# Background products in halves of 64 rows beside the scores, transfers issued at due times, and the end of the program on other engines

## The chip, the cores and the metric

One Trainium2 core runs the program. TensorE (PE in the rows) multiplies, with its weight loads shown apart as PEld; VectorE (DVE), ScalarE (ACT) and GpSimd (POOL) work beside it, and SyncE (SP) issues every transfer from one in-order queue. The metric is the device time of one execution in microseconds, lower is better.

## The reference

One transformer block with adaptive layer norm over 2048 rows of width 512 in float32. `mod` is cut into six rows of 512.

```python
mod = (silu(c) @ w_mod).reshape(1, 6, 1, -1)
sa, ca, ga, sb, cb, gb = (mod[:, i] for i in range(6))
h = layernorm(x) * (1 + ca) + sa
x = x + ga * A(h)     # 32 heads of 16: softmax(q k^T / 4) v, then @ wo
h = layernorm(x) * (1 + cb) + sb
x = x + gb * B(h)     # gelu_tanh(h @ w1 + b1) @ w2 + b2, w1 512 x 1792
```

## The kernel before

Projections keep float32 accuracy by three products of split operands (high x high, low x high, high x low, `terms3`), each 128x128 weights by 512 columns in the one-pass float32 format. A prologue takes the modulation, the first norm, the values and the first part of queries and keys. q and k go through HBM as high and low parts and come back with a head in 48 rows, two heads of a group in rows 0 to 47 and 64 to 111. Two more rows hold the row maximum, so that `e` comes out shifted.

The scores loop runs over 32 units `u` (4 query blocks of 512 by 8 groups of 4 heads) of 16 key chunks, 512 steps in all. A step has four `exp_mm` (L533: `e`, 50 rows on one half of the array, to banks 0 to 2; ScalarE's exponential, L539, empties them) and four `mx_mm` (L375: scores with query rows out, on the other half, to banks 3 to 5; VectorE's maximum, L380, empties them), which run 96 products ahead for the maxima of the next units. `max_rows` (L386) turns a unit's maxima and sends them through `m_d` (L394) into the rows of `qst`. `pv_step` (L555) multiplies with the values in four tiles of 32 columns side by side into bank 6. The order is written out by hand: CYCLE has 12 `Y` (an `e` and an `mx`), three `p` (a `pv` step) and two `b` (background products).

Background products (L283, bank 7, 128 rows) come from generators: `block0`, the remaining q and k projections with `load_w` and `split_w` of their weights, then `ffn_block` for each query block: 4 groups of 12 products with `wo`, norm, transposes, 14 `ffn1` groups of 12 with a GELU written out on GpSimd around a tanh on ScalarE, and `ffn2` groups. `bg` issues four or six at a time:

```python
            elif o == "b":
                nb += 1
                bg(6 if work and len(work) <= NB and nb % 2 else 4)
```

`prep` splits the weights of the feed-forward part and stores them in HBM during the first units. `o_prep` (L584) divides a finished part of the attention by its sums: load `dn` and `ob`, reciprocal, store, load `rb` over the rows, multiply and split on GpSimd. `later(n, f)` calls `f` at the n-th tick; one tick is one `Y`, or after the loop three background products. A transfer stands in SyncE's queue where the program text issues it, and waits there for its data. After the loop the last query block's `ffn_block` runs alone.

## Time and profile before

| | |
|---|---|
| median of 3 runs | 2231.18 us (2221.09 to 2232.93) |
| profiled execution | 2227.8 us, span 2225.6 us, mean granted clock 0.917 |
| TensorE busy | 1925.6 us, 87% |
| VectorE busy | 1412.5 us, 63% |
| ScalarE busy | 1235.2 us, 56% |
| GpSimd busy | 751.7 us, 34% |
| transfers | 242.45 MB |

Busy time of TensorE counts overlapping products once. Where the engine waits and for whom is read by stage: prologue to 161.54 us (first `e`), loop to 2012.20 us (last `pv`), end of the program to 2225.60 us.

### The profile page before, as it was taken

To read this page: it belongs to the slowest core of one execution; us is meant where nothing else is said; L and a number is where in the kernel's file an instruction comes from. 1 tells how busy PE (TensorE), PEld (TensorE's weight loads), DVE (VectorE), ACT (ScalarE), POOL (GpSimd) and SP (SyncE) were. 2 spreads that over 40 slices of the span, in tenths; PEclk is the share of its full clock that TensorE was granted. 3 is DMA by queue.
4 is the path that set the end of the run, shared out by engine and by line. 5 is a ranking of instruction groups with operands and counts; after the bars stand their busy time and mean duration, and the time that the engine had idled before them with its cause. 6 is when DMAs were issued, how large, how long until landed. Compare 5 with 4: busy or idle time off the path is not lost.

```text
span 2225.6 us, 29467 instructions
## 1 busy us (share of the span) xinstructions
PE 1925.6 (87%) x10544; PEld 855.4 (38%) x10544; DVE 1412.5 (63%) x2317; ACT 1235.2 (56%) x2302; POOL 751.7 (34%) x787
## 2 busy tenths in 40 slices
PE   7899949898799898999979999999889999995566
PEld 5543313343233343433333333333333334333344
DVE  4476727687578777777767777778687777601000
ACT  2316637576466675767556766656557667571110
POOL 3313332321100451523302523414215415151886
PEclk8998969999789999999989999999899999996777
DMA  7554665556323443424443434333542524123221
GB/s 231 157 137 126 177 182 141 175 141 191 78 59 76 94 92 88 105 63 85 96 145 81 84 80 120 83 82 80 182 101 52 113 78 101 43 69 136 92 95 47
DMA packets 123919, 242.45 MB, mean 109 GB/s; under 512 B 32134, under 2 KB 51606, under 8 KB 123774
## 3 DMA queue, kind: packets, MB, share of 16 engines
q1 hardware_dynamic: 123774, 240.57, 41.5%
q8 instruction: 84, 1.38, 0.3%
q14 instruction: 61, 0.50, 0.1%
HBM read 187.61 MB, written 52.90 MB: 108 GB/s over the span
## 4 chain that ended last, share of the span: by engine, by line
PE 67%; DMA 10%; POOL 8%; DVE 6%; ACT 4%; issue 3%; SPq 2%; POOLq 0%; DVEq 0%; ACTq 0%
PE pv L562 20%; PE bg L283 19%; PE e L533 18%; PE mx L375 8%; DVE mxp L380 3%; PE pr L283 2%; DMA wf<-in_B_w_dram 2%; DMA w<-w1s 2%; ACT p L539 1%; DMA dn<-ou 1%; DMA wraw<-in_A_wqkv_dram 1%; DVE y L712 1%; DMA rden<-dn 1%; POOL h L692 1%; ACT h L683 1%
## 5 line engine op out<-in xcount | busy, mean ns | idle before, releaser
L380 DVE TENSOR_REDUCE mxp<-mx 128x1 f32<-128x512 f32 x2048 | 1298.8, 685 | 449.4 <-PE mx L375 388.4
L539 ACT ACTIVATE p<-e 128x512 f32<-128x512 f32 x2048 | 1092.7, 599 | 611.4 <-PE mx L375 399.9
L375 PE MATMUL mx<-kh,qst 48*128 48x512 f32 x2048 | 742.3, 459 | 51.1 <-DVE mxp L380 45.9
L533 PE MATMUL e<-qst,kh 50*128 50x512 f32 x2048 | 733.5, 453 | 15.4 <-ACT p L539 14.4
L562 PE MATMUL pv<-p,vg 128*32 128x512 f32 x4096 | 577.0, 637 | 6.2 <-ACT osb L548 6.2
L533 PEld LDWEIGHTS e<-qst,kh 50*128 50x128 f32 x2048 | 329.8, 192 | 616.3 <-ACT p L539 465.1
L375 PEld LDWEIGHTS mx<-kh,qst 48*128 48x128 f32 x2048 | 326.3, 192 | 88.6 <-DVE mxp L380 76.0
L283 PE MATMUL bg<-w,g 128*128 128x512 f32 x672 | 212.3, 443 | 89.1 <-POOL g L693 47.9
L283 PE MATMUL bg<-pc,w 128*128 128x512 f32 x672 | 193.8, 420 | 26.3 <-ACT h L683 16.3
L283 PEld LDWEIGHTS bg<-w,g 128*128 128x128 f32 x672 | 124.4, 201 | 168.8 <-POOL g L693 53.3
L713 POOL TENSOR_TENSOR x<-x,y 128x512 f32<-128x512 f32 x48 | 61.4, 1282 | 295.7 <-DVE y L712 295.6
L562 PEld LDWEIGHTS pv<-p,vg 128*32 128x32 f32 x4096 | 82.5, 110 | 198.2 <-issue 180.2
L283 PEld LDWEIGHTS bg<-pc,w 128*128 128x128 f32 x672 | 118.4, 191 | 94.2 <-issue 34.0
L712 DVE TENSOR_TENSOR y<-bg,gb_b 128x512 f32<-128x512 f32 x48 | 32.9, 685 | 181.3 <-PE bg L283 176.8
L691 POOL TENSOR_TENSOR u<-u,h 128x512 f32<-128x512 f32 x56 | 71.8, 1283 | 136.7 <-ACT u L689 136.7
L684 POOL TENSOR_TENSOR u<-h 128x512 f32<-128x512 f32 x56 | 58.3, 1041 | 112.7 <-ACT h L683 112.5
L599 POOL TENSOR_TENSOR ob<-ob,rb 128x512 f32<-128x512 f32 x16 | 20.4, 1274 | 224.4 <-DMA rb<-rden 205.3
L283 PE MATMUL bg<-wo,pc 128*128 128x512 f32 x192 | 60.9, 449 | 37.7 <-POOL pc L600 24.0
L683 ACT ACTIVATE h<-bg,b_h 128x512 f32<-128x512 f32 x56 | 38.7, 691 | 97.4 <-PE bg L283 80.3
L283 PE MATMUL bg<-hThi,wqk 128*128 128x512 f32 x176 | 59.0, 460 | 34.7 <-ACT wqk L163 23.3
L686 POOL TENSOR_TENSOR u<-u,h 128x512 f32<-128x512 f32 x56 | 71.7, 1281 | 4.7
L692 POOL TENSOR_TENSOR h<-u,h 128x512 f32<-128x512 f32 x56 | 71.6, 1278 | 4.4
(100 smaller groups left out, 949.9 us busy)
## 6 DMA issues: line engine op xcount, KB each, us to landing
kh<-qk SPq DMA_DIRECT2D x366, 128.0 KB
w<-w1s SPq DMA_DIRECT2D x56, 512.0 KB
w<-w2s SPq DMA_DIRECT2D x56, 512.0 KB
vg<-v SPq DMA_DIRECT2D x32, 664.0 KB
qk<-parts SPq DMA_DIRECT2D x32, 512.0 KB
qst<-qk SPq DMA_DIRECT2D x192, 64.0 KB
ou<-osb SPq DMA_DIRECT2D x32, 256.0 KB
wo<-wos SPq DMA_DIRECT2D x16, 512.0 KB
```

The source lines that it names most:

```text
L283: te.matmul(ps, p, q, start=i == 0, stop=i == len(terms) - 1)
L375: te.matmul(ps, qst[u][r0 : r0 + KR, p, qc * P : (qc + 1) * P], kh(u, kr // 2)[r0 : r0 + KR, p, (kr % 2) * TB : (kr % 2 + 1) * TB], start= ...
L380: ve.tensor_reduce(mxp[u][:, hc, kr : kr + 1], ps, axis=AX.X, op=ALU.max, negate=True)
L533: te.matmul(ps, kh(u, kc // 8)[r0 : r0 + KX, p, (kc % 8) * P : (kc % 8 + 1) * P], qst[u][r0 : r0 + KX, p], start=True, stop=True)
L539: ac.activation(pt[n], ps, AF.Exp, scale=SCALE)
L562: te.matmul(cur["ps"][32 * j : 32 * (j + 1)], vg[u][:, kc, j * VW : j * VW + 32], pt.pop(4 * s + j), start=kc == 0, stop=kc == NKC - 1)
L683: ac.activation(h, ps, AF.Identity, scale=0.5, bias=b1_h[:, i : i + 1])
L684: gp.tensor_tensor(s, h, h, op=ALU.mult)
L686: gp.tensor_tensor(s, s, h, op=ALU.mult)
L691: gp.tensor_tensor(s, s, h, op=ALU.mult)
L692: gp.tensor_tensor(h, s, h, op=ALU.add)
L713: gp.tensor_tensor(x2[t], x2[t], y, op=ALU.add)
```

## The change

A background product is cut into two products of 64 rows (`bg_mm`) that add to the same bank. In `half_step`, one per step, six of them on half `h` alternate with scores on the other half, three `mx` and three `e`; then one pair of an `e` and an `mx`, then one `pv` step. The half changes with each step, and a group of 12 products takes four steps. As both halves add to one bank, the first product on the other half is made to wait (`add_manual_dep`) for the first ScalarE exponential or copy that was issued after the last one of the old half (`saw`). CYCLE and `bg` go. A tick is now one `e`, or one pair before the loop, or two products after it.

The weights of the last two q and k parts are loaded and split inside `block0`, in two buffers in place of three. The stores of parts, maxima, weights, attention and output, and the steps of `o_prep`, get due times by `later`. `w2` is stored times `gb`, so the multiplication on VectorE and the addition on GpSimd become one addition on VectorE. The weight ring has 8 buffers and reloads a slot when its tile has been used; the exponential's tiles are 12 in place of 9.

After the loop seven banks hold background groups. What is left of the third block's work alternates with the last block, which has tiles of its own, prepares its attention output on VectorE, two parts at a time, and takes GELU as one ScalarE function with VectorE's subtraction for the low part.

```diff
-CYCLE = ("Y", "Y", "Y", "p", "Y", "Y", "b", "Y", "Y", "Y", "b", "Y", "Y", "p", "Y", "Y", "p")
-PARTS = ((0, 5), (5, 10), (10, NF))
-MM = "mm"
+AFTER = mybir.DependencyInfo(mybir.DependencyClass.Sync, mybir.DependencyReason.DATA)
+RUN = 6
+WB = 8
+PARTS = ((0, 6), (6, 12), (12, NF))
+AHEAD = 2
+GELU_A = 0.7978845608028654
+GELU_C = 4 * 0.044715
...
+    def mm(ps, term, i, n, r=slice(None)):
+        return te.matmul(ps, term[0][r], term[1][r], start=i == 0, stop=i == n - 1)
+
...
-            store_qk(w, k, b, parts)
+            if bk == "bg":
+                later(8, lambda: store_qk(w, k, b, parts))
+            else:
+                store_qk(w, k, b, parts)
...
-        sy.dma_start(m_d[u], m2.bitcast(F32))
...
+        def load():
+            mrows.add(u)
...
+        later(5, lambda: sy.dma_start(m_d[u], m2.bitcast(F32)))
+        later(11, load)
...
-    ppcm, ppool = pool("p", bufs=9)
+    ppcm, ppool = pool("p", bufs=12)
...
-    wcm2, wpool2 = pool("wqk2", side="right")
-    wq.append(wpool2.tile([P, 2, 2, KC, P], FR, name="wqk2"))
-    load_w(2)
-    split_w(2)
...
-            sy.dma_start(dst, t.bitcast(F32))
-
-        return rest
+            later(7, lambda: sy.dma_start(dst, t.bitcast(F32)))
+
+        later(11, rest)
...
-        preps.append((w2[f * P : (f + 1) * P, :], w2_d[f], None))
+        preps.append((w2[f * P : (f + 1) * P, :], w2_d[f], gb_b))
...
+    def exp_mm(a):
+
+        s, p = divmod(ec[a], 2)
...
+        ec[a] += 1
...
+            t = ppool.tile([P, TB], F32, tag="p", name="p")
+            saw(ac.activation(t, ps, AF.Exp, scale=SCALE))
+            pt[4 * s + p * 2 + a] = t
+            advance()
...
+        saw(ac.activation(o, pv, AF.Copy))
+        later(2, lambda: sy.dma_start(ou_d[qb][g], o))
...
+            later(8, lambda: ready.append((qb, g // 2)))
...
+        tgt = pools["pc"][k] if b < NB - 1 else pools["tail"]["pc"][k]
+        eng = gp if b < NB - 1 else ve
+        r = rden_d[b][k * 8 : (k + 1) * 8]
+        busy[0] += 1
+
+        def inv():
...
+            later(1, store)
+
+        def store():
+            sy.dma_start(r.rearrange("h (a f) -> (h a) f", f=32), dn)
+            later(4, load)
+
+        def load():
+            sy.dma_start(rb, bass.AP(tensor=r.tensor, offset=r.offset, ap=[[TB, 8], [0, DH], [1, TB]]))
+            later(4, div)
...
         def div():
-            ve.reciprocal(dn, dn)
-            sy.dma_start(rden_d[b][k * 8 : (k + 1) * 8].rearrange("h (a f) -> (h a) f", f=32), dn)
-            r = rden_d[b][k * 8 : (k + 1) * 8]
...
-            gp.tensor_tensor(ob, ob, rb, op=ALU.mult)
-            gp.tensor_copy(tgt[:, 0], ob)
-            gp.tensor_tensor(tgt[:, 1], ob, tgt[:, 0].bitcast(F32), op=ALU.subtract)
-            done[b] = k
-            busy[0] = False
-
-        busy[0] = True
-        later(8, div)
+            eng.tensor_tensor(ob, ob, rb, op=ALU.mult)
+            eng.tensor_copy(tgt[:, 0], ob)
+            eng.tensor_tensor(tgt[:, 1], ob, tgt[:, 0].bitcast(F32), op=ALU.subtract)
+            done[b] += 1
+            busy[0] -= 1
+
+        later(5, inv)
...
+        if not ready or "f" not in pools:
+            return
+        last = ready[0][0] == NB - 1
+        if "tail" in pools if last else free_pc[0] >= ready[0][0]:
+            if busy[0] < 1 + last:
+                o_prep(*ready.pop(0))
+
+    def until(cond):
+        while not cond():
+            yield None
+
+    def wait(n):
+        t0 = clock["t"]
+        return until(lambda: clock["t"] >= t0 + n)
...
+    def ffn_block(b):
...
+        def wload():
+            while n[0] < len(seq) and (n[0] < WB or seq[n[0] - WB] in used):
+                key = seq[n[0]]
+                t = f.tile([P, 2, D], FR, tag="w", name=f"w{key[0]}", bufs=WB)
...
+        if not tail:
+            wload()
...
-        while done[b] < KC - 1:
-            yield lambda: done[b] == KC - 1
-        t0 = clock["t"]
-        yield lambda: clock["t"] >= t0 + 12
+        yield from until(lambda: done[b] == KC - 1)
+        yield from wait(5)
...
+            yield [(pc[i][:, a, sl], wt["o", i][:, w]) for i in range(KC) for a, w in three], "bg", evac
+        if not tail:
+            used.update(seq[:KC])
+            wload()
+        yield from wait(2)
...
+        yield from wait(2)
...
+        yield from wait(4)
...
+            h = tmp("h32")
...
+            eng = ve if tail and fc % 2 else gp
+            eng.tensor_copy(pc[fc][:, 0], h)
+            eng.tensor_tensor(pc[fc][:, 1], h, pc[fc][:, 0].bitcast(F32), op=ALU.subtract)
+
+        for fc in range(KC):
+            yield lambda fc=fc: trans(fc)
+        if tail:
+            yield "ffn"
+            wload()
+        else:
+            yield from wait(4)
...
+            def evac_tail(ps):
+                h = tmp("h")
+                ac.activation(h, ps, AF.Gelu_apprx_tanh, bias=b1_f[:, i : i + 1])
+                g = f.tile([P, 2, TB], FR, tag="g", name="g", bufs=8)
+                ac.activation(g[:, 0], h, AF.Copy)
+                ve.tensor_tensor(g[:, 1], h, g[:, 0].bitcast(F32), op=ALU.subtract)
+                gt[i] = g, clock["t"] - 9
...
 
                 def second():
...
+                    ac.activation(s, s, AF.Tanh, scale=2 * GELU_A)
+                    g = f.tile([P, 2, TB], FR, tag="g", name="g", bufs=8)
+                    gp.tensor_scalar(s, s, 1.0, None, op0=ALU.add)
+                    gp.tensor_tensor(h, s, h, op=ALU.mult)
+                    gp.tensor_copy(g[:, 0], h)
+                    gp.tensor_tensor(g[:, 1], h, g[:, 0].bitcast(F32), op=ALU.subtract)
+                    gt[i] = g, clock["t"]
+
+                later(10, second)
+
...
+        for first, lo, hi in parts:
...
+                yield ffn1(i)
+                used.add((1, i))
+                wload()
...
+            yield from until(lambda: all(i in gt and clock["t"] >= gt[i][1] + 9 for i in range(lo, hi)))
...
-                    y = tmp("y")
-                    ve.tensor_tensor(y, ps, gb_b, op=ALU.mult)
-                    gp.tensor_tensor(x2[t], x2[t], y, op=ALU.add)
+                    ve.tensor_tensor(x2[t], ps, x2[t], op=ALU.add)
...
+                        later(2, lambda: sy.dma_start(out[r0 : r0 + P, :], x2[t]))
...
+                yield [(gt[i][0][:, a, sl], wt[2, i][:, w]) for i in range(lo, hi) for a, w in three], "bg", evac
+            used.update((2, i) for i in range(lo, hi))
+            wload()
+        yield from wait(3)
...
+        load_w(2)
+        yield from q(0, range(1, NB))
+        split_w(2)
+        yield from wait(6)
+        load_w(3)
+        yield from kq(2)
+        yield from q(1, range(1, NB))
+        split_w(3)
+        yield from wait(6)
+        yield from kq(3)
+        yield from q(2, range(1, NB))
+        yield from q(3, range(1, NB))
+        yield from until(lambda: not preps and not any(hooks.values()))
         open_ffn()
...
+    def work():
+        yield from block0()
+        for b in range(NB - 1):
+            yield from ffn_block(b)
+
...
+    def saw(ins):
+
+        if act["g"] and not act["g"]["seen"]:
+            act["g"]["seen"] = ins.ins
...
+    def bg_mm(h):
+
+        g = act["g"]
+        terms, bk, evac = g["group"]
...
+        if g["n"] == 0:
+            g["ps"] = take(bk)
+        ins = mm(g["ps"], terms[i], g["n"], 2 * len(terms), slice(h * 64, h * 64 + 64)).ins
+        if g["n"] and g["half"] != h:
+            tc.add_manual_dep(ins, g["seen"].name, AFTER, reason="both halves of the rows add to one bank")
+        g["half"], g["seen"] = h, None
+        g["at"][h] += 1
+        g["n"] += 1
+        if g["n"] == 2 * len(terms):
+            evac(g["ps"])
+            act["g"] = None
+        return act["g"] is not None
+
+    def half_step(hs):
+        h = hs % 2
+        if act["g"] is None:
+            j = next(jobs, None)
+            if callable(j):
+                j()
+            elif j is not None:
+                act["g"] = {"group": j, "at": [0, 0], "n": 0, "seen": None}
+        nx = min(64 * NU, LEAD + 4 * (hs + 1))
+        ne = 4 * (hs + 1)
+
+        def x_ok(a):
+            return sum(xc) < nx and xc[a] < 32 * NU
+
+        def e_ok(a):
+            return sum(ec) < ne and ec[a] < 2 * NU * NKC
+
+        more = act["g"] is not None
+        k = 0
+        while more and k < RUN:
+            a = 1 - h
+            more = bg_mm(h)
+            if e_ok(a) and sum(ec) < ne - 1 and (k % 2 == 1 or not x_ok(a)):
+                exp_mm(a)()
+            elif x_ok(a):
+                mx_mm(a)()
+            k += 1
+        while sum(ec) < ne or sum(xc) < nx:
+            a = 0 if ec[0] <= ec[1] else 1
+            fs = []
+            if sum(ec) < ne:
+                fs.append(exp_mm(a))
+                if x_ok(1 - a):
+                    fs.append(mx_mm(1 - a))
+                elif e_ok(1 - a):
+                    fs.append(exp_mm(1 - a))
             else:
...
+                fs += [mx_mm(i) for i in range(2) if x_ok(i)]
+            for f in fs:
+                f()
+        if hs:
+            assert min(ec) >= 2 * cur["pv"] + 2
+            pv_step()
+
...
         u, kc = divmod(s, NKC)
-        if kc == 0 and u + 2 < NU:
+        if kc == 1 and u + 2 < NU:
...
-        if kc == 1 and u + 2 < NU:
+        if kc == 2 and u + 2 < NU:
...
-        if kc == 8 and u + 2 < NU:
+        if kc == 9 and u + 2 < NU:
...
+        if preps and s % 3 == 2:
+            prep(*preps.pop(0))
...
+    for hs in range(NU * NKC):
+        half_step(hs)
+    if act["g"]:
+        while bg_mm(1 - hs % 2):
+            pass
+    pv_step()
+    while act["g"]:
+        bg_mm(hs % 2)
     close(ppcm, vgcm, kqcm2)
...
+    ring("bg", (0, 1, 2, 3, 4, 5, 7))
+    tcm, tpool = pool("tail")
+    pools["tail"] = {"pc": [tpool.tile([P, 2, TB], FR, name=f"pct{i}") for i in range(KC)],
+                     "x2": [tpool.tile([P, D], F32, name=f"x2t{i}") for i in range(4)],
+                     "w": {}}
+    for key, src in [(("o", k), wo_d[k]) for k in range(KC)] + [((1, i), w1_d[i]) for i in range(2)]:
+        t = tpool.tile([P, 2, D], FR, name=f"wt{key[0]}{key[1]}")
+        sy.dma_start(t.bitcast(F32), src)
+        pools["tail"]["w"][key] = t
+    b1_f = tpool.tile([P, NF], F32, name="b1_f")
+    gp.tensor_scalar(b1_f, b1_h, 2.0, None, op0=ALU.mult)
+
+    def do(j):
...
+        elif j is not None:
+            run(j, 2, advance)
+        else:
+            advance()
...
+    last = ffn_block(NB - 1)
+    left, j = True, None
+    while left or j != "ffn":
+        if j != "ffn":
+            j = next(last)
+            if j is not None and j != "ffn":
+                do(j)
+                continue
+        i = next(jobs, 0)
+        left = left and i != 0
+        do(i if left else None)
+    for j in last:
+        do(j)
+    for _ in range(4):
         advance()
```

## Rows read from the trace of the kernel before

**Rows 1.** Windows of three stages: busy PE, PEld, DVE, ACT, POOL; clock; DMA share

```profile
0.00:161.54 161.54, 138.21 (x585) 87.28 (x585) 89.44 (x170) 43.36 (x67) 46.39 (x68) 0.93 0.57 171
161.54:2012.20 1850.66, 1662.49 (x9544) 679.12 (x9542) 1302.73 (x2116) 1170.58 (x2202) 568.56 (x591) 0.94 0.42 105
2012.20:2225.60 213.40, 124.85 (x418) 88.97 (x418) 20.30 (x32) 21.28 (x33) 136.75 (x128) 0.72 0.27 95
```

**Rows 2.** Windows of L533 alone (two), then of L283 alone: busy, clock, DMA

```profile
600.20:647.80 47.60, 25.56 (x65) 11.37 (x64) 0.89 0.34 62
703.20:1961.90 1258.70, 498.15 (x1407) 224.21 (x1407) 0.96 0.39 94
...
703.20:1961.90 1258.70, 323.42 (x1062) 180.76 (x1062) 0.96 0.39 94
```

**Rows 3.** Timeline of PE, 1641.5 to 1646.4 us: start, duration, operation, count

```profile
1641.62 0.50 PE L533 MATMUL e<-qst,kh 50*128 50x512 f32 x1
...
1642.51 1.06 PE L562 MATMUL pv<-p,vg 128*32 128x512 f32 x8
...
1643.51 0.50 PE L533 MATMUL e<-qst,kh 50*128 50x512 f32 x1
...
1644.18 1.66 PE L283 MATMUL bg<-wo,pc 128*128 128x512 f32 x6
...
1645.77 0.50 PE L533 MATMUL e<-qst,kh 50*128 50x512 f32 x1
```

**Rows 4.** Chain that ended last, 100 to 110 us: start, duration, what

```profile
102.50 6.65 PE pr L283 x28
```

**Rows 5.** Waits of PE, 700 to 1960 us: total, times, longest

```profile
PE bg L283 <- DVE y L712: 38.5, 28, 2.3
PE mx L375 <- DVE mxp L380: 22.0, 10, 10.4
PE bg L283 <- ACT h L683: 21.9, 24, 1.1
```

**Rows 6.** Chain that ended last, 160 to 173 us

```profile
162.06 8.34 DMA wraw<-in_A_wqkv_dram
```

**Rows 7.** Waits of PE, 161 to 700 us

```profile
PE bg L283 <- ACT wqk L163: 23.3, 1, 23.3
```

**Rows 8.** Waits of SyncE's queue, whole span

```profile
SPq L394 <- POOL m L393: 377.4, 28, 26.6
```

**Rows 9.** Waits of all engines, whole span

```profile
DVE dn L595 <- DMA dn<-ou: 102.5, 11, 26.2
```

**Rows 10.** Timeline of all engines, 1641.5 to 1646.4 us

```profile
1646.31 0.60 ACT L539 ACTIVATE p<-e 128x512 f32<-128x512 f32 x1 [1.18 <-PE mx L375]
1646.34 0.69 DVE L380 TENSOR_REDUCE mxp<-mx 128x1 f32<-128x512 f32 x1 [0.97 <-PE mx L375]
```

**Rows 11.** The page's costliest groups: count, busy us, mean ns, idle before

```profile
L380 DVE TENSOR_REDUCE mxp<-mx 128x1 f32<-128x512 f32 x2048 | 1298.8, 685 | 449.4 <-PE mx L375 388.4
L539 ACT ACTIVATE p<-e 128x512 f32<-128x512 f32 x2048 | 1092.7, 599 | 611.4 <-PE mx L375 399.9
```

**Rows 12.** Groups by line, whole span

```profile
L683 ACT ACTIVATE h<-bg,b_h 128x512 f32<-128x512 f32 x56 | 38.7, 691 | 97.4 <-PE bg L283 80.3 <-POOL g L694 16.8
...
L182 ACT ACT_TABLE_LOAD x1 | 1.3, 1283 | 0.7 <-PEq L838 0.7
```

**Rows 13.** Chain that ended last, 2012 us to the end

```profile
2021.48 8.68 DMA w<-w1s
2030.17 8.23 DMA dn<-ou
...
2040.33 3.80 DMA rb<-rden
...
2058.81 0.70 DVE x L647
...
2074.28 7.17 PE bg L283 x18
```

More of the change, by code (lines that the diff above doesn't have):

```diff
@@ L277, in advance, with run @@
             f()
-    def group(bk, terms, evac):
+    def mm(ps, term, i, n, r=slice(None)):
+        return te.matmul(ps, term[0][r], term[1][r], start=i == 0, stop=i == n - 1)
+    def run(group, every=0, f=None):
+        terms, bk, evac = group
         ps = take(bk)
-        for i, (p, q) in enumerate(terms):
-            te.matmul(ps, p, q, start=i == 0, stop=i == len(terms) - 1)
+        for i, t in enumerate(terms):
+            mm(ps, t, i, len(terms))
             if i == len(terms) - 1:
                 evac(ps)
-            yield MM
+            if f and i % every == every - 1:
+                f()
     def terms3(ahi, alo, bhi, blo):
@@ L327, in proj_v @@
         n = range(KC)
-        yield from group(bk, [(hi[:, i, sl], wv[:, j, i]) for i in n for j in range(2)]
-                         + [(lo[:, i, sl], wv[:, 0, i]) for i in n], evac)
+        return [(hi[:, i, sl], wv[:, j, i]) for i in n for j in range(2)] + [(lo[:, i, sl], wv[:, 0, i]) for i in n], bk, evac
     qst, mxp = {}, {}
@@ L342, in load_k @@
     def load_k(u, h, t0=0, t1=HS):
+        assert all((1, u % NG // 2, b) in stored for b in range(2 * h + t0 // TB, 2 * h + t1 // TB))
         for i, part in enumerate((0, 0, 1)):
@@ L355, in load_q @@
         qb, g = divmod(u, NG)
+        assert (0, g // 2, qb) in stored
         qst[u] = kqpool.tile([P, 2, TB], FR, tag="qst", name="qst", bufs=3)
@@ L426, in block_kernel @@
     load_w(1)
-    def run(gen, every=0, f=None):
-        for n, _ in enumerate(gen):
-            if f and n % every == every - 1:
-                f()
     def mx_some(n, upto):
         for _ in range(n):
-            if mi[0] < upto:
+            if sum(xc) < upto:
                 mx_pair()
@@ L571, in open_ffn @@
     def open_ffn():
+        assert not preps and not any(hooks)
         close(*pools["old"])
@@ L605, in o_prep @@
-        busy[0] = True
-        later(8, div)
-    def try_prep():
-        if ready and pools.get("f") and free_pc[0] >= ready[0][0] and not busy[0]:
-            o_prep(*ready.pop(0))
-    def weights(b):
-        seq = [("o", k) for k in range(KC)] + [(1, f) for f in range(6)] + [(2, f) for f in range(5)]
-        seq += [(1, f) for f in range(6, 11)] + [(2, f) for f in range(5, 10)]
-        seq += [(1, f) for f in range(11, NF)] + [(2, f) for f in range(10, NF)]
-        return seq
-    def ffn_block(b, last=False):
-        f = pools["f"]
-        x2, xn, pc = pools["x2"], pools["xn"], pools["pc"]
-        seq = weights(b)
-        wt, nl = {}, [0]
-        def wload(upto):
-            while nl[0] <= min(upto, len(seq) - 1):
-                key = seq[nl[0]]
-                t = f.tile([P, 2, D], FR, tag="w", name=f"w{key[0]}", bufs=9)
+        tgt = pools["pc"][k] if b < NB - 1 else pools["tail"]["pc"][k]
@@ L696, in evac @@
-                later(9, second)
-            n = range(KC)
-            w = w.rearrange("p a (k n) -> p a k n", n=P)
-            yield from group("bg", terms3([w[:, 0, k] for k in n], [w[:, 1, k] for k in n],
-                                          [pc[k][:, 0] for k in n], [pc[k][:, 1] for k in n]), evac)
-        def ffn2(lo, hi):
-            wload(seq.index((2, lo)) + 8)
-            t1 = clock["t"]
-            yield lambda: all(i in gt for i in range(lo, hi))
+                    ac.activation(s, s, AF.Tanh, scale=2 * GELU_A)
@@ L710, in evac @@
                 def evac(ps, t=t):
-                    y = tmp("y")
-                    ve.tensor_tensor(y, ps, gb_b, op=ALU.mult)
-                    gp.tensor_tensor(x2[t], x2[t], y, op=ALU.add)
+                    ve.tensor_tensor(x2[t], ps, x2[t], op=ALU.add)
                     if hi == NF:
                         r0 = b * TB + t * P
-                        sy.dma_start(out[r0 : r0 + P, :], x2[t])
-                yield from group("bg", [(gt[i][:, a, sl], wt[2, i][:, w]) for i in range(lo, hi)
-                                        for a, w in ((0, 0), (0, 1), (1, 0))], evac)
@@ L747, in block0 @@
-        for k in (1, 2, 3):
-            for b in range(1, NB):
-                yield from proj_qk("bg", 0, k, b)
-        open_ffn()
-    pools["old"] = [wcm2, scm, wcm, hcm]
-    work = [block0()] + [None] * NB
-    hold = [None]
-    def bg(n):
-        while n > 0 and work:
-            if hold[0]:
-                if not hold[0]():
-                    return
-                hold[0] = None
-            if work[0] is None:
-                b = NB - len(work)
-                work[0] = ffn_block(b)
-            r = next(work[0], None)
-            if r is None:
-                work.pop(0)
-            elif r is MM:
-                n -= 1
-            else:
-                hold[0] = r
```

213 lines of the change are left out of this document (84 added, 129 removed).

## The prediction

> **What bounds the kernel now.** I read the windows of the three stages first: the reader is to see which stage holds the time and which engine is busy in it [rows 1]. The profiled execution took 2227.8 us: a span of 2225.6 and 2.2 around it, 3.4 under the median of 2231.18. The scores loop has 1850.66 us for 512 steps of four `e` products, four `mx` products and one `pv`, 3.61 us a step; the prologue has 161.54 and the end of the program 213.40.
>
> Second, windows of single lines in a long stretch of the loop, for the steps that it holds [rows 2]: 1407 `e` products are 352 steps in 1258.70 us, 3.58 us each, with 1062 background products, 3.02 a step. Third, the timeline of TensorE, for its bursts from start to start [rows 3]. Three pairs of `e` and `mx` take 0.89 us, two take 0.67. The two products of a pair sit on different 64-row halves and run side by side, so a pair costs little more than one full-width product, which is 6.65/28 = 0.2375 us in a run of 28 [rows 4]. I take 0.24 a pair and what is left, 0.18, as the entry of a burst with another tiling. Six full-width products take 1.59, that is 6 x 0.2375 and an entry of 0.165. The `pv` step takes 1.00, entry included. One pass of CYCLE (three steps) is 12 pairs in five bursts, 3.78; three `pv`, 3.00; nine full-width products in two bursts, 2.48: together 9.26, or 3.09 us a step.
>
> The other engines need less: VectorE is busy 1302.73 us in the loop, 2.54 a step, ScalarE 1170.58, 2.29 [rows 1]. So TensorE sets the step, and 3.58 - 3.09 = 0.49 us of it is lost. The table of waits names most: 38.5 + 22.0 + 21.9 = 82.4 us for the one `bg` bank to be emptied by VectorE or ScalarE and for `mx` banks [rows 5], 0.23 a step. The mean granted clock of 0.96 [rows 2] hides at most 0.04 x 1258.7 = 50 us at the 1.2 GHz level, 0.14 a step.
>
> Last I read the chain that ended last and the waits of single engines, for plain stops in the loop. The first exponential stands behind `split_w(2)` on ScalarE, whose data takes 8.34 us [rows 6]; `split_w(3)` stops TensorE for 23.3 [rows 7]. SyncE, in order, stood 377.4 us at the issue of `m_d` with later transfers queued behind it [rows 8]. VectorE stood 102.5 us at the reciprocal for `dn` with the reduces queued behind [rows 9].
>
> At the end TensorE has 124.85 us of work at a clock of 0.72, GpSimd 136.75 [rows 1]: the GELU chain on GpSimd and, ahead of it, a chain of small transfers.
>
> **The products in halves.** A background product becomes two of 64 rows, each beside a score on the other half. Six halves and eight scores fill seven slots: 7 x 0.24 + 0.18 + 1.00 = 2.86 us a step with three products, against 3.09. The streaming is the same (four pairs and three products before, seven pairs after); the 0.23 is entries saved. No row shows such a product beside a score; the price of a slot is bounded by 0.2375 [rows 4] and by 0.67/2 = 0.335, a two-pair burst with its entry counted in [rows 3]. I take 0.24, as three pairs at 0.89 fit it.
>
> **The new wait.** The first product on the other half waits for the first exponential behind the last one of the old half; behind it stand all later products, the scores of the next step too. An exponential begins 0.54 us after its product, a reduce 0.57 [rows 10], and they follow one another at 1092.7/2048 = 0.534 and 1298.8/2048 = 0.634 us [rows 11]. With `e` in slots 1, 3, 5 and 6, the third exponential ends near 0.34 + 0.54 + 3 x 0.534 = 2.48 us, the change comes at 2.86: hidden, with 0.38 to spare. A pass of 0.69 us of another kind ahead of it on ScalarE [rows 12], the tanh of one group in four steps, makes it 0.31 late: 0.08 a step. The emptying of `bg` had the next product right behind it; now a pair and `pv` come between. ScalarE's is hidden by them. VectorE's add waits for three reduces, 0.57 + 3 x 0.634 + 0.69 = 3.16, 0.30 late on 12 of a block's some 137 steps: 0.03. Together some 0.10 where 0.23 stood. For the clock I keep 0.10 of the 0.14. The multiplication by `gb_b` moves into the stored weights: one GpSimd pass less per group and the same VectorE pass. So 3.06 us a step with products.
>
> **How many such steps.** `block0` has 22 groups of 24 halves, 88 steps, and ends near step 102 when the weights are prepared (32 at one in three steps). The first block starts near step 136 (its attention ends at 128, then the due times) and has 128 steps of products and 9 without, so the second starts near 273 and the third near 412, of which 90 steps of products fit. That is 88 + 256 + 90 = 434; 78 have scores alone, for which TensorE needs 2.14 us and VectorE 4 x 0.634 = 2.54. I take 2.75; such a stretch took 2.97 before, at a clock of 0.89 [rows 2].
>
> **The DMAs.** Removed: 8.34 us and 23.3 us of stops; the weights are now loaded 12 and more steps ahead. Every issue moved to its due time takes it out of SyncE's way: the 377 us at `m_d` held `kh`, `qst`, `ou` and `w` behind it. What stays: with `open_ffn` eight `w` and four `x` loads go out just ahead of a `dn`, and the reciprocal on VectorE waits with the reduces behind it. Such a load took 8.68 us to land [rows 13], and the first weights of a block are wanted two steps after issue. I take 25 us for four such places; the bounds are nothing and the 102.5 us that VectorE stood before [rows 9].
>
> Loop: 434 x 3.06 + 78 x 2.75 + 25 = 1328 + 215 + 25 = 1568 us.
>
> **The end.** 114 products of the third block (384 less 90 x 3) are left over, and the fourth's 384. All four `o_prep` of the last block now begin here, two at a time on VectorE. From the chain at the end [rows 13]: loads 8.68, `dn` 8.23, `rb` 3.80, and with the reciprocal's store between and three VectorE passes some 25 us, and 8 for the second pair: 33 us, beside which 114 x 0.24 = 27 us of left-over work is mostly done. Then 48 products of `wo`, 11.5; the norm and the transposes, 15.5 before from the add on `x` to the next product [rows 13] and 14 with VectorE sharing the splitting; 336 products, 81; the last add and store, 4.5. Sum 144, and 3 for clock lost to the stops: 147. Gelu on ScalarE is not in the trace; bounded by nothing and by two passes of 0.69 a group, it hides under 12 products, 2.85 us, and a table load is 1.28 [rows 12]. The weights of the end are 13.6 MB in 81 us, 168 GB/s; 95 GB/s took a share of 0.27 [rows 1], so they fit. If the cover fails at both places the end takes 165; if all hides, 135.
>
> **Sum.** 161.5 + 1568 + 147 + 2.2 = 1879 us.
>
> **Rivals.**
> *The losses stay.* TensorE is in order, so a score held by its bank now holds products too, and VectorE is used 2.54 of 3.06. If the lost 0.49 a step remains: 2.86 + 0.49 = 3.35, loop 434 x 3.35 + 240 = 1694, total 2005. For it: the 38.5 us at the bank, and every engine nearer its limit. Against it: the emptying of `bg` gets a pair and `pv` as cover that it did not have.
>
> *Halves pack less well in long runs.* Runs of more than three pairs were never free of waits. At 0.335 a slot the step is 1.00 + 7 x 0.335 + 0.20 = 3.55, loop 1781, total 2091. Against it: the third pair of a burst cost 0.22 more than the second. The Trainium skill's "TensorE: Matmul & The Clock Gate", Part 3, "Measured speedup vs the span model", measured 3.07 times for four row tiles instead of four; carried over as an estimate, a slot would be 0.24 x 4/3.07 = 0.31, and the total about 2100. The two-pair and three-pair rows speak against it here.
>
> *The halves do not run beside the scores (slower).* If a product and the score after it follow one another, the six shared slots cost 0.24 more each: 2.86 + 1.44 + 0.20 = 4.50, loop 2193, total 2504. It decides from a step of (2225.6 - 161.5 - 147 - 240)/434 = 3.86, that is when more than 3.3 of the six fail to overlap. For it: the product adds up in a bank over many instructions, as no score does. Against it: `e` and `mx` on these same halves overlap [rows 3].
>
> *Everything hides.* 2.86 and 2.60 us a step, no stop, an end of 135: 1444 + 161.5 + 135 + 2.2 = 1743.
>
> **How the numbers follow.** Chances: the forecast (1800 to 1960) 0.60, the losses stay (to 2050) 0.17, bad packing 0.08, all hides 0.08, no overlap 0.05, and 0.02 for a mixture that ends within 0.5% of 2231, about what a measurement here can tell from no change. So faster 0.93, same 0.02, slower 0.05. The range, 1790 to 2095, takes in the first two rivals and leaves out 0.08 below and 0.07 above.
>
> **What would show it.** Right: `e` and `mx` at about 3.0 us a step; each product line twice as often with 64 rows, starting with a score; `pv` the only tiling change; SyncE's wait at `m_d` near nothing; no 23 us gap; an end near 147 us with GpSimd nearly idle in its last two thirds. Wrong: products waiting on ScalarE's `p` at each change of half (the new wait is not hidden); `mx` banks as TensorE's longest wait, with VectorE above nine tenths (the losses stay); slots of 0.3 us without a wait (packing); stops at `dn` of more than 25 us in all; a half-rate clock in the steps without products.

## The result, and the profile after

1942.40 us, median of 4 runs (1937.71 to 1942.81), against 2232.05 for the kernel before (2221.09 to 2233.46): a ratio of 0.8707, 95% interval 0.8676 to 0.8738, faster. The forecast was 1879 in a range of 1790 to 2095, 63 us too low. The profiled execution took 1942.59 us, its span 1940.80.

The windows of the three stages of the kernel after, in the columns of [rows 1]:

```profile
0.00:169.58 169.58, 145.32 (x588) 91.52 (x590) 90.05 (x171) 43.88 (x68) 47.60 (x69) 0.89 0.55 166
169.58:1790.90 1621.32, 1514.05 (x10730) 717.51 (x10730) 1272.75 (x2106) 1142.57 (x2195) 521.82 (x542) 0.96 0.61 142
1790.90:1940.80 149.90, 129.41 (x542) 100.80 (x542) 45.51 (x71) 27.24 (x41) 32.99 (x30) 0.93 0.43 157
```

The loop fell from 1850.66 to 1621.32 us (summed: 1568), the end from 213.40 to 149.90 (147), with GpSimd's work there from 136.75 to 32.99; the prologue rose to 169.58 (161.5). The edge at 1790.90 lies at the last `pv` but one; the last ends at 1795.83. Cut there, as the rows of [rows 1] are, the loop has 1626.25 us and the end 144.97. The DMA share says that something else came with it: 0.61 in the loop, 0.42 before.

**The step.** One step of the loop on the timeline of TensorE of the kernel after (start, duration, operation, count), between two `pv` steps:

```profile
1231.70 0.50 PE L285 MATMUL bg<-pc,w 64*128 64x512 f32 x1
1231.70 0.50 PE L391 MATMUL mx<-kh,qst 48*128 48x512 f32 x1
1232.03 0.39 PE L285 MATMUL bg<-pc,w 64*128 64x512 f32 x1
1232.04 0.39 PE L552 MATMUL e<-qst,kh 50*128 50x512 f32 x1
...
1232.98 0.71 PE L552 MATMUL e<-qst,kh 50*128 50x512 f32 x2
1233.21 0.47 PE L391 MATMUL mx<-kh,qst 48*128 48x512 f32 x1
1233.62 1.07 PE L581 MATMUL pv<-p,vg 128*32 128x512 f32 x8
1234.61 0.49 PE L285 MATMUL bg<-pc,w 64*128 64x512 f32 x1
```

Each half starts with the score beside it. From slot to slot it is 0.33 for the first and then (1233.21 - 1232.03)/5 = 0.236 us; seven slots take 1.92, `pv` 0.99, the step 2.91. The windows of L552 alone in a stretch without a stop hold 128 products, 32 steps, at the 2.4 GHz level: 93.30/32 = 2.92 us a step. The step with its losses had been summed at 3.06.

```profile
1173.70:1267.00 93.30, 47.71 (x128) 23.79 (x128) 1.00 0.47 110
```

**The stops.** Waits of TensorE inside the loop of the kernel after (169.6 to 1790.9 us), then of VectorE there (us in total, times, longest):

```profile
PE mx L391 <- DVE mxp L396: 61.2, 12, 25.0
PE e L552 <- ACT p L557: 17.7, 64, 1.0
PE bg L285 <- DMA wo<-wos: 8.6, 1, 8.6
...
PE bg L285 <- ACT p L557: 1.2, 4, 0.3
```

```profile
DVE dn L617 <- DMA dn<-ou: 61.6, 8, 25.4
```

The new wait of a half for its exponential, the last line of the first fence, is hidden: 1.2 us in the whole loop. The emptying of `bg`, 38.5 us by VectorE alone in [rows 5], is no longer among the first. What TensorE waits for is VectorE, 61.2 us in 12 waits, and VectorE in turn for the loads ahead of a `dn`, 61.6. The two timelines around the longest of these stops, VectorE's and then TensorE's (releaser in brackets), and the window over it:

```profile
492.75 0.35 DVE L617 RECIPROCAL dn<-dn 128x32 f32<-128x32 f32 x1 [25.44 <-DMA dn<-ou]
493.02 2.42 DVE L396 TENSOR_REDUCE mxp<-mx 128x1 f32<-128x512 f32 x4
```

```profile
468.19 0.50 PE L552 MATMUL e<-qst,kh 50*128 50x512 f32 x1 [0.20 <-ACT p L557]
493.70 0.79 PE L391 MATMUL mx<-kh,qst 48*128 48x512 f32 x1 [25.02 <-DVE mxp L396]
```

```profile
469.00:496.30 27.30, 2.60 (x11) 0.52 0.80 282
```

The reduces stand behind the reciprocal on VectorE, the `mx` products behind the reduces, everything else behind those; the DMA share over the stop is 0.80.

**The queue.** Waits of SyncE's queue over the whole span of the kernel after (L362 is the load of `kh`, L677 that of the weight ring's `w`):

```profile
SPq L362 <- PE mx L391: 136.8, 50, 17.3
SPq L677 <- PE mx L391: 125.0, 33, 11.7
SPq L362 <- DMA kh<-qk: 99.8, 132, 4.6
SPq L422 <- POOL m L410: 89.5, 14, 16.5
...
SPq L503 <- DMA vg<-v: 59.5, 17, 5.1
```

The issues of two tiles (count, KB each), of the kernel after and then of the kernel before:

```profile
kh<-qk SPq DMA_DIRECT2D x558, 128.0 KB
vg<-v SPq DMA_DIRECT2D x49, 664.0 KB
```

```profile
kh<-qk SPq DMA_DIRECT2D x366, 128.0 KB
```

The wait at `m_d` (L422) fell from 377.4 us [rows 8] to 89.5; it had been forecast near nothing. The two longest waits are for TensorE; the run with loads once has them too (175.1 and 132.0 us). What is new is that `kh` goes out 558 times in place of 366, `vg` 49 times in place of 32, and that 242.45 MB became 281.34. A second load into the same tile waits for the first, 99.8 us in 132 waits for `kh`, in the queue in which `dn` stands too. SyncE's issues about the longest stop (455 to 494 us) show the order, with both loads of `qst` in one row and then the `dn` for which VectorE waits:

```profile
464.50 10.72 SPq L377 DMA_DIRECT2D qst<-qk  x12
...
485.53 0.66 SPq L607 DMA_DIRECT2D dn<-ou  x1
```

VectorE had been idle since 467.3; the `dn` went out at 485.53 and had landed 7 us later. With loads once it went out at 474.82 and had landed 6 us later. So this stop was spent in the queue far more than in the transfer, in spite of the DMA share of 0.80; for the other stops the two were not told apart.

### The profile page after: what moved, and what is told of

Its sections match the earlier page's. It is cut to its first block, busy times and chain, and to the rows that moved or that the text cites. A ratio compares the mean times of both kernels' runs of the same rounds, so it can differ in the third digit from the quotient of the medians.

```text
span 1940.8 us, 32415 instructions
## 1 busy us (share of the span) xinstructions
PE 1788.8 (92%) x11852; PEld 909.8 (47%) x11852; DVE 1408.3 (73%) x2347; ACT 1213.7 (63%) x2303; POOL 602.4 (31%) x640
## 2 busy tenths in 40 slices
DMA packets 137036, 281.34 MB, mean 145 GB/s; under 512 B 35958, under 2 KB 55430, under 8 KB 136878
## 4 chain that ended last, share of the span: by engine, by line
PE 75%; DMA 9%; DVE 7%; ACT 3%; POOL 2%; SPq 2%; issue 1%; DVEq 0%; ACTq 0%; POOLq 0%
PE bg L285 34%; PE pv L581 23%; PE e L552 10%; PE mx L391 4%; DVE mxp L396 4%; PE pr L285 3%; DMA kh<-qk 2%; DMA dn<-ou 2%; ACT p L557 1%; DMA rb<-rden 1%; SPq L362 1%; DVE x L774 1%; DMA qst<-qk 1%; DVE bst L225 1%; SPq L377 1%
## 5 line engine op out<-in xcount | busy, mean ns | idle before, releaser
L391 PE MATMUL mx<-kh,qst 48*128 48x512 f32 x2048 | 879.0, 453 | 68.5 <-DVE mxp L396 61.5
L552 PE MATMUL e<-qst,kh 50*128 50x512 f32 x2048 | 763.8, 427 | 17.7 <-ACT p L557 17.7
L552 PEld LDWEIGHTS e<-qst,kh 50*128 50x128 f32 x2048 | 379.7, 190 | 217.3 <-ACT p L557 194.7
L285 PE MATMUL bg<-w,g 64*128 64x512 f32 (+1 forms) x1080 | 293.1, 410 | 10.5 <-DVE x L774 6.1
L285 PE MATMUL bg<-pc,w 64*128 64x512 f32 (+1 forms) x996 | 273.9, 408 | 2.4 <-ACT p L557 0.9
L285 PEld LDWEIGHTS bg<-w,g 64*128 64x128 f32 (+1 forms) x1080 | 193.1, 189 | 159.8 <-ACT p L557 79.7
L285 PEld LDWEIGHTS bg<-pc,w 64*128 64x128 f32 (+1 forms) x996 | 171.4, 184 | 163.9 <-ACT p L557 100.0
L285 PE MATMUL bg<-hThi,wqk 64*128 64x512 f32 x352 | 109.3, 431 | 1.8 <-POOL wqk L168 1.6
L748 POOL TENSOR_SCALAR s<-s 128x512 f32<-128x512 f32 x42 | 63.0, 1501 | 132.1 <-ACT s L746 124.1
L285 PEld LDWEIGHTS bg<-hThi,wqk 64*128 64x128 f32 x352 | 61.3, 193 | 82.8 <-ACT p L557 70.9
L285 PE MATMUL bg<-wo,pc 64*128 64x512 f32 x288 | 84.1, 420 | 9.7 <-DMA wo<-wos 8.6
L285 PEld LDWEIGHTS bg<-wo,pc 64*128 64x128 f32 x288 | 50.7, 189 | 58.4 <-ACT p L557 28.7
```

The costliest lines, as they stand in the source:

```text
L285: return te.matmul(ps, term[0][r], term[1][r], start=i == 0, stop=i == n - 1)
L391: te.matmul(ps, qst[u][r0 : r0 + KR, p, qc * P : (qc + 1) * P], kh(u, kr // 2)[r0 : r0 + KR, p, (kr % 2) * TB : (kr % 2 + 1) * TB], start= ...
L552: te.matmul(ps, kh(u, kc // 8)[r0 : r0 + KX, p, (kc % 8) * P : (kc % 8 + 1) * P], qst[u][r0 : r0 + KX, p], start=True, stop=True)
L748: gp.tensor_scalar(s, s, 1.0, None, op0=ALU.add)
```

## The experiments

All times are medians against the kernel before on the same chip (2229 to 2236 us); "after" is the 1942.40 us.

**Loads once.** In `exp_mm` the step's loads are started by the product that finds itself the least advanced. If the first lane goes first in a step, the second finds the same and starts them again.

```diff
+    started = set()
...
-        if min(ec) == ec[a] and ec[a] % 2 == 0 and (a == 0 or ec[0] > ec[1]):
+        if min(ec) == ec[a] and s not in started:
+            started.add(s)
```

> step_start called once for each step; in the changed kernel it is called twice for about half of them, so that K, V and q loads go out twice (281.34 MB in place of 242.45). Theory A, the doubled loads hold SyncE's queue and the transfers behind it (dn, wo, qst late): traffic back to about 242 MB, the SyncE waits at kh on its own earlier load (99.8 us) and at vg (59.5) gone, VectorE's wait at dn in the loop from 61 us to under 25, time 1942 to about 1870. Rival B, the reciprocal's due time of five ticks is too short whatever the traffic: the wait at dn stays above 45 us, time at or over 1925.

Measured: 1873.97 us (ratio 0.8402, 0.8377 to 0.8427), 68 under after, with 242.62 MB. The loop's window and VectorE's wait for `dn` in it:

```profile
164.46:1721.70 1557.24, 1496.24 (x10742) 712.00 (x10739) 1270.72 (x2106) 1142.14 (x2196) 522.49 (x543) 0.98 0.49 122
```

```profile
DVE dn L619 <- DMA dn<-ou: 21.6, 5, 15.8
```

That is the forecast of the first theory in time, traffic and wait. The loop is 1557 us where 1568 was summed; the step without a stop stays at 2.92 (186.60 us for 64 steps). The doubled loads made about half of the stops' cost: 64 of the 68 us are in the loop. A part of that is clock: TensorE's busy time in the loop falls from 1514.05 to 1496.24 us, at a granted clock of 0.98 in place of 0.96.

**Divisors later.** The doubled loads stay; the reciprocal comes 16 ticks behind its load in place of 5.

```diff
-        later(5, inv)
+        later(16, inv)
```

> The changed kernel with the reciprocal due 16 ticks after the load of dn in place of 5, doubled loads left in. Theory A: VectorE's wait at dn in the loop falls from 61 us to under 10, but the late queue shows again at wo or rb; time about 1900. Rival B, the due time is the cause: all stops of the loop go, time about 1860.

Measured: 1892.85 us (0.8491, 0.846 to 0.8522), 50 under after and near the first theory's 1900; VectorE's wait for `dn` in the loop fell from 61.6 to 24.3 us, not under 10. `kh` still goes out 522 times, 36 fewer than in after, so a little of the gain is traffic. So the stops cost through VectorE, which is in order: the same late load harms less if VectorE comes to it later.

**Both.** The two edits together.

> step_start once for each step and the reciprocal due 16 ticks after the load of dn. If the two act at one place each (doubled loads on SyncE's queue, reciprocal ahead of its data on VectorE): VectorE's wait at dn in the loop under 5 us (25 with the first alone), no stop over 5 us in the loop, time 1874 to about 1850. Rival, the first edit already took all that the second could: 1874 within 6.

Measured: 1859.21 us (0.8322, 0.8293 to 0.835): 15 more than the first edit alone brings, 9 over the forecast's 1850. A stop of 7.5 us ahead of a `dn` stayed where none over 5 was expected, and of 18 us gained in the loop the end gives 7 back (151.74 us against 144.77). The gains, 68 and 50, don't add up, as both go for the same stops.

**Full-width products, all together.** Background products of 128 rows without halves, three at the start of the step and the four pairs behind them.

```diff
...
-        while more and k < RUN:
-            a = 1 - h
+        while more and k < RUN // 2:
             more = bg_mm(h)
-            if e_ok(a) and sum(ec) < ne - 1 and (k % 2 == 1 or not x_ok(a)):
-                exp_mm(a)()
-            elif x_ok(a):
-                mx_mm(a)()
```

> The changed kernel with background products of 128 rows, three ahead of the four pairs of each step, no halves and no wait between them; all else the same. By the sum (the halves save one entry of a burst): 0.16 us more in each of 434 steps, 70 us, about 2010. Rival, the halves save waits of the score banks as well: 0.4 us a step and more, 2110 or over. Rival, the halves bring nothing and the due times all: 1942 within 10.

Measured: 2317.77 us (1.039, 1.0359 to 1.0421), slower than the kernel before, far over the sum's 2010 and on the side of the first rival (2110 or over). The timeline of TensorE, one step:

```profile
1402.04 0.98 PE L285 MATMUL bg<-pc,w 128*128 128x512 f32 x3
1402.94 0.49 PE L552 MATMUL e<-qst,kh 50*128 50x512 f32 x1
1402.95 0.73 PE L391 MATMUL mx<-kh,qst 48*128 48x512 f32 x2
...
1404.12 0.49 PE L552 MATMUL e<-qst,kh 50*128 50x512 f32 x1 [0.21 <-ACT p L557]
1404.26 0.50 PE L391 MATMUL mx<-kh,qst 48*128 48x512 f32 x1
1404.68 1.06 PE L581 MATMUL pv<-p,vg 128*32 128x512 f32 x8
```

The step is 3.64 us, from 1402.04 to 1405.68. Three banks take three `e`; the fourth starts 1.18 after the first, where three slots are 0.7, because it waits for ScalarE, and `pv` waits behind it. This kernel also sends every step's loads twice (322.56 MB), so it tells the halves' worth badly.

**Full-width products between pairs.** The same three products, now between two pairs and two pairs; the store of parts is due after 6 ticks in place of 8.

```diff
...
+        def three():
+            for _ in range(RUN // 2):
+                if not (act["g"] and bg_mm(h)):
+                    break
...
+            if n == 2:
+                three()
+            n += 1
```

> Full-width products as in the run before with products ahead of the four pairs, but in the middle of the step, two pairs ahead and two behind, so that no run of scores is longer than the banks hold (the stores of parts are due two ticks earlier). Theory, the fourth pair waited for a bank of the exponential: step 0.67 + 0.88 + 0.67 + 1.00 = 3.22 us against 2.92 with halves, 0.30 in 434 steps, 130 us, about 2070. Rival, full-width products cost waits of another kind: step 3.5 or over, 2200 and more.

Measured: 2178.45 us (0.9747, 0.9705 to 0.9789), with the forecast step of 3.22 us where nothing stops, but 108 us over the forecast time: the loads are doubled (322.56 MB), with stops of up to 20 us.

**The same, loads once** (and the store of parts due after 8).

> The background products are of 128 rows again, three of them between two pairs of score products and the other two pairs, and PV behind them; each step's loads go out once. Theory (halves beside the scores save the array's time alone, and the stops come from loads that go out twice): the step of this order measured 3.22 us against 2.92 with halves, so 434 steps cost .30 more each, 130 us, and the whole is 1874 + 130 = about 2004 us (1985 to 2025), with traffic back at about 243 MB. Rival (the stops of the full-width order have a cause of their own, its stores and its bursts): the loads going out once take off no more than some 40 us of the 2178, and it stays above 2100.

Measured: 2003.28 us (0.8966, 0.8934 to 0.8998), the forecast to 1 us. Its timeline of TensorE, one step:

```profile
1303.44 1.06 PE L583 MATMUL pv<-p,vg 128*32 128x512 f32 x8
1304.44 0.50 PE L554 MATMUL e<-qst,kh 50*128 50x512 f32 x1
...
1305.11 0.96 PE L285 MATMUL bg<-w,g 128*128 128x512 f32 x3
1306.00 0.49 PE L554 MATMUL e<-qst,kh 50*128 50x512 f32 x1
...
1306.66 0.64 PE L583 MATMUL pv<-p,vg 128*32 128x512 f32 x4
```

1.00 + 0.67 + 0.89 + 0.66 = 3.22. The streaming is that of the step of 2.91; what the halves save is two entries of a burst, 0.30 us. Over 434 steps that is 130 us, and the runs give 2003.28 - 1873.97 = 129.

**Waiting for the last exponential.** `saw` keeps the last ScalarE work of the old half instead of the first, so that the change of half waits longer.

```diff
-        if act["g"] and not act["g"]["seen"]:
+        if act["g"]:
```

> The changed kernel, but the first product on the other half waits for the last exponential issued since the old half, not for the first. Theory, the new wait is hidden with some 0.4 us to spare and the last exponential ends about when the next step begins: each change of half then waits 0.1 us and, with tanh or an evacuation in ScalarE's queue, up to 0.8; three of four steps with products, 40 to 130 us, 1985 to 2070. Rival, TensorE never stands at this wait in either form: 1942 within 10.

Measured: 1967.83 us (0.8802, 0.8764 to 0.884), 25 over after, under the forecast's 1985 to 2070. The window of L552, 32 steps as for after above, gives 96.80/32 = 3.02 us a step:

```profile
1183.10:1279.90 96.80, 47.58 (x128) 23.76 (x128) 1.00 0.48 107
```

By the starts of its steps, most of those with the wait are 0.04 us longer and two are 0.8; that makes the mean of 0.10. So even the last exponential is mostly 0.04 us late. The first ends one ScalarE pass (0.60 us) earlier, which by estimate leaves it some 0.5 us to spare where the prediction had 0.38.

**GELU of the last block on GpSimd.** The last block takes the written-out GELU of the others.

```diff
-                          [pc[j][:, 0] for j in k], [pc[j][:, 1] for j in k]), "bg", evac_tail if tail else evac
+                          [pc[j][:, 0] for j in k], [pc[j][:, 1] for j in k]), "bg", evac
```

> The changed kernel with the written-out GELU on GpSimd in the last block as well, everything else of the end left. Theory, GpSimd is the bound of the end again: 14 groups of some 7.5 us of passes, 105 us against 81 of TensorE; the end grows from 150 to about 180 us, time about 1972. Rival, the other parts of the end (seven banks, left-over work, VectorE for the attention) brought its gain: within 10 us of 1942.

Measured: 1990.83 us (0.8922, 0.8891 to 0.8952), 48 over after and 19 over the forecast. Waits of TensorE in the end of the program:

```profile
PE bg L285 <- POOL g L750: 40.2, 8, 6.2
```

**Due times undone.** Loads once, and every store, row and step of `o_prep` issued where the kernel before issued it; then two parts of that alone, the rows of `m_d` and `qst`, and the stores. The steps of `o_prep` are undone in the first run only. What the expectations call the row of divisors is `m_d`, which holds the maxima.

```diff
...
-        later(5, lambda: sy.dma_start(m_d[u], m2.bitcast(F32)))
-        later(11, load)
+        sy.dma_start(m_d[u], m2.bitcast(F32))
+        load()
...
-        later(2, lambda: sy.dma_start(ou_d[qb][g], o))
+        sy.dma_start(ou_d[qb][g], o)
...
```

> As the run with loads that go out once (1874 us), with every due time of the change undone: rows of divisors and queries, the stores of parts, of rows and of outputs and the last projection's start are issued where the kernel before issued them. Theory A (due times keep SyncE's queue from waiting, and a waiting queue is what the loads behind it suffer from): SyncE's wait at the row of divisors comes back towards the 377 us of the kernel before, and the loop gets several stops of 3 to 10 us, 1900 to 1930 us. Rival (the loads are issued early enough to bear a waiting queue): within 10 us of 1874.

> As the run with loads that go out once (1874 us), with the rows of divisors and queries alone issued where the kernel before issued them. With all due times undone it was 1965 us, 91 more, and SyncE waited 255.2 us at this row. Theory A (the row that waits for GpSimd is what holds the queue, as the prediction had it): most of the 91 comes back, 1930 to 1960 us, with SyncE's wait at the row about 250 us. Rival (another due time carries it): within 20 us of 1874.

> As the run with loads that go out once (1874 us), with the stores alone issued where the kernel before issued them: parts of queries and keys, prepared weights, attention output, rows of the result. With all due times undone SyncE waited 298.1 us at the attention's store and 110.3 at the prepared weights. Theory A (the row of divisors carries the 91 us): within 25 us of 1874. Rival (a wait is a wait, wherever it stands): 40 to 80 us more, in proportion to SyncE's waits at the stores, 1915 to 1955 us.

Measured: all undone 1965.47 us (0.8801, 0.877 to 0.8832), 91 more than with loads once; the rows alone 1928.77 (0.8656, 0.863 to 0.8683), 55 more; the stores alone 1913.68 (0.8592, 0.8558 to 0.8626), 40 more. The first is over its forecast (1900 to 1930), the second lies 1 us under the first theory's 1930 to 1960, the third 1 us under the rival's 1915 to 1955 and out of its first theory's. With every due time undone SyncE waits, over the whole span:

```profile
SPq L569 <- ACT osb L568: 298.1, 25, 24.5
SPq L419 <- POOL m L407: 255.2, 25, 20.8
SPq L522 <- POOL wsp L521: 110.3, 22, 9.6
```

with the rows alone, and with the stores alone:

```profile
SPq L422 <- POOL m L410: 358.0, 31, 25.4
```

```profile
SPq L572 <- ACT osb L571: 259.4, 27, 17.9
```

55 and 40 make 95, near the 91. The wait at `m_d` with the rows alone is 358.0 us where 250 was expected. The forecast that this row carries it was half right: the stores, which no sentence of the prediction priced, are worth nearly as much. The step without a stop is still 2.90 (the window of L551, 64 steps, with all undone):

```profile
711.70:897.40 185.70, 93.61 (x257) 47.58 (x256) 1.00 0.51 110
```

So the 91 is not in the step but about the stops, and the largest part ahead of `dn`: TensorE's waits for VectorE's reduces are 71.2 us in the loop against 29.6 with loads once. Further waits came at `wqk` (10.5), `kh` (8.3) and `wo` (4.8), TensorE's busy time is 29 us longer at a granted clock of 0.95 against 0.98, and the end is 8 longer.

**Divisors at their own time in each block.** Loads once, and 24 ticks in the first block, 16 in the next two, 5 in the last.

```diff
-        later(5, inv)
+        later(5 if b == NB - 1 else 16 if b else 24, inv)
```

> As the run with loads that go out once, with the divisor's inversion due 24 steps later in the first block, 16 in the ones between and 5 in the last. Theory (the gap of 7 us behind the first block's end and that of 6 us behind the loop's end in the 1859 us run are both VectorE or GpSimd held at the inversion, too early in the first block and too late in the last): both go, and 1859 becomes 1846 to 1853. Rival (what follows takes their place, and the end is a chain that the inversion only moves within): within 6 us of 1859.

Measured: 1861.01 us (0.8326, 0.8302 to 0.8349), no different from 1859.21, as the rival had it; 1846 to 1853 was forecast. Neither gap went: the end has 151.72 us as in the run with both edits (151.74), and in the first block the timeline of VectorE shows the wait here, and then in the run with both edits:

```profile
484.89 0.35 DVE L619 RECIPROCAL dn<-dn 128x32 f32<-128x32 f32 x1 [6.82 <-DMA dn<-ou]
```

```profile
475.16 0.35 DVE L619 RECIPROCAL dn<-dn 128x32 f32<-128x32 f32 x1 [7.46 <-DMA dn<-ou]
```

Eight ticks more moved the reciprocal by 9.7 us, of which 4.8 is the later start of this execution's loop (167.39 against 162.55). SyncE issued the load 5.4 us later, and it took some 10 us to land in place of 5.7. Why it took longer was not settled.

## Why the prediction was right, and where it was off

**The sum.** The traces hold 2598 recorded halves in the loop, 433 steps with products, against 434 counted. By terms, measured less summed: the steps 434 x (2.92 - 3.06) = -61 us, the lone-score steps nothing (44.0 us for the 16 of one unit, 2.75 each), the prologue +8, the end +3. The loop has 1621 - 434 x 2.92 - 78 x 2.75 = 140 us beside its steps where 25 were summed: +115. Together +65, of which the profiled executions show 1942.6 - 1879 = 64. Cut at the last `pv` itself, 5 us move from the end to the loop: +120 and -2. That the total came so near is in part luck: the over-sized step paid for half of the stops.

**Packing.** 0.24 a slot was right, at 0.236. The rival by 0.335 is out. The Trainium skill's "TensorE: Matmul & The Clock Gate", Part 3, "Measured speedup vs the span model", whose 3.07 of 4 gave an estimate of 0.31 a slot, does not carry over from its four tiles to the two halves: in this case's trace seven slots in a row show no such loss. The total of about 2100 that the prediction put on that estimate does not follow from its own sum: 1.00 + 7 x 0.31 + 0.20 = 3.37 a step gives about 2013.

**What the halves save.** The prediction said that entries alone are saved, 0.23 a step against an average of the old bursts. Against a step of its own three products it is 0.30, shown by the two runs with loads once: 129 us. The rest, from 3.58 [rows 2] to 3.22, compares a mean with a step without a stop. In the stretch of [rows 2] a quarter of the passes of CYCLE (from every 12th `e` to the next, most with ten products, not nine) take 9.52 us or less, 3.17 a step; in the run with full-width products and loads once the 432 steps with products have a mean of 3.28. So what the new order without halves saves is waits and not streaming, and how much of that the order brings and how much the due times, no run shows. That the order matters is shown: with the same products but the scores bunched the step was 3.64.

**The step's losses: the term that was over-sized.** 0.10 for waits and 0.10 for the clock were added to 2.86. Measured are 2.91 to 2.92 in a stretch at a granted clock of 1.00: no clock loss in such a step, and some 0.06 of entries and waits. Over the whole loop the clock was 0.96. Steps without products do not lower it by themselves: a stretch of them had 1.00 (542.02 to 586.06 us), another, with a stop at its start, 0.50 (596.6 to 617.1). The argument by cover held: bank and exponential both have a pair and `pv` in front of the next product, and the run that waits for the last exponential puts the cover at some 0.5 us.

**The stops: the term that failed.** "25 us for four such places" was 140 us of stops and small waits, and the upper bound, the 102.5 us of [rows 9], was under it. The failed step was one of reading: the count of issues. The prediction took the loads to go out as often as before; that the new order starts a step's loads from two lanes, and for `kh` in 32 of 60 cases twice (192 more issues, six to a load), it did not reckon with. Cut at the last `pv` the 140 are 145: 67 went with the second loads, and 18 more with a later reciprocal. The sign that the prediction itself had named, stops at `dn` of more than 25 us, came at 61.6. The mechanism named for the stops, loads just ahead of `dn` with reduces behind them on VectorE, was the right one, and the run that moved only the reciprocal shows it. With both edits some 60 us are left. About 26 of them belong to the norm of the three blocks, for which the sum had no term: four `xn` passes on VectorE (L709, 3.82 us in a row at 637.90) hold the reduces, so that the step takes 5.8 to 6.4 us, and the 12 steps with transposes behind them take 49.6 us where 12 x 2.75 = 33 were summed. A last stop ahead of a `dn` has 8, and the first unit 4 (50.9 us against the 46.7 of the next). The rest, some 22, is not settled.

**Due times.** Their direction was right, and they are worth 91 us on the kernel with loads once. The prediction named them and gave them no term.

**The end.** 149.9 us against 147, or 145.0 from the last `pv`. The chain that ended last in the kernel after:

```profile
1827.51 3.52 DMA rden<-dn
...
1836.15 13.23 PE bg L285 x51
1849.41 0.69 DVE x L774
...
1859.55 77.56 PE bg L285 x332
```

From the end of the last `pv` at 1795.83 to the projection it is 40 us (33 summed), then 13.2 (11.5), 10.1 for norm and transposes (14), 77.6 for the products (81), and the last add and store. Errors of both signs cancel. With GELU on GpSimd the program is 48 us longer and the end has 197.1 us: 40.2 are TensorE's waits for GpSimd, and 11 are longer busy time at a granted clock of 0.82 against 0.93. That part of the change is worth more than the forecast of the run.

**The other rivals.** No overlap is out by the timeline. Losses that stay (2005) happened to lie as near as the forecast, but not by its mechanism: ScalarE's banks held TensorE for 17.7 us in 64 waits. Of the prologue's 8 us some 5 belong to the execution: with loads once, which leaves the prologue alone, it was 164.46, and in the other variants of the changed kernel between 162.4 and 167.4.

## What to carry to other kernels

Count the issues of each tile in the new trace before anything else: a condition that starts loads "once a step" from two lanes cost 68 us here. If an in-order engine takes a small load's data ahead of work that TensorE needs, give the load its distance on the queue and the engine its distance behind it; each mends part of the same stop, so their gains don't add. In steps without a stop, an order in which scores of few banks are spread was worth more (3.64 to 3.22) than the packing itself (3.22 to 2.92). Compare such steps with such steps: against the mean of the old loop the new order seems to save streaming, and it saves waits.

## What the runs showed of the hardware

A 64-row product beside a 50-row or 48-row one on the other half costs 0.236 us a slot in runs of seven, though one of them adds up in its bank over 24 products. A second load into a tile whose first load is under way holds SyncE's queue: 99.8 us in 132 waits for `kh`, none of them with loads once. In the 27.3 us over the longest stop TensorE had 2.60 us of work and the granted clock was 0.52, the 1.2 GHz level; the next unit (542.02 to 586.06 us) ran at 1.00.
